# Masks in the slot of the scores, another order of the first transfers, and ScalarE's rounding of outputs ahead of weights

## The chip, the cores and the metric

The kernel runs on one core of one Trainium2 chip. The metric is the device time of one execution in microseconds (us); the median of three runs of the kernel before is 1189.74 us. Five engines work beside each other, each through its own instructions in order: TensorE (PE; its weight loads stand apart as PEld), VectorE (DVE), ScalarE (ACT), GpSimd (POOL) and SyncE (SP), which issues nearly all transfers.

## The reference

A retention layer is followed by two feed-forward layers:

```python
state = gamma * state + outer(k[t], v[t])      # per batch and head, 768 steps
y[t]  = scale * q[t] @ state
x  = y of 4 batches as 3072 tokens x 512
h  = x @ w_in   (512 x 2048);  g = h - tanh(h);                 x = g @ w_out
h  = x @ w_in2  (512 x 2048);  g = h if h > 0 else exp(h) - 1;  out = g @ w_out2
```

The weights arrive as 64-bit floats. The kernel reads each as two 32-bit words and makes a 32-bit float of them on the chip.

## The kernel before

**Retention.** The 3072 tokens are cut into 24 steps of 128 tokens; step s belongs to batch element s mod 4 and to chunk s // 4. For each step TensorE makes the scores of keys and queries into two PSUM banks (`att_scores`, L164), VectorE multiplies them by a causal mask with decay (L173, two instructions, tile `pt`) and, from chunk 1 on, scales the queries in place (`att_scale_q`, L135, tile `qk`). Then TensorE makes the outputs `o` (`att_out`): from chunk 1 on it first multiplies the scaled queries by the state (L187), then the masked scores by the values (L195). The result is split into a rounded half (ScalarE, L203) and a rest (VectorE, L204). The state is renewed by TensorE (L214, from keys that VectorE scaled, L149, tile `kn`) and VectorE (L237, L240; for chunk 0 one copy for two steps, L228). The outputs and the state's product use PSUM banks `a0` and `a1` that the scores of the next step use too.

**Feed-forward.** One iteration n handles one block of 512 tokens and one of 16 slices f of the hidden width. TensorE makes h by 12 matmuls (L251); ScalarE and VectorE turn h into v by a chain (ScalarE L271, L272, L274, L275; VectorE L277, L280, L283, L284 in the first layer); the next iteration splits v into g (ScalarE L260, VectorE L264); two iterations later TensorE adds the 12 matmuls of the second product (L317, `acc`).

**Weights.** A weight tile is fetched (L81, tile `raw`), ScalarE makes a float of its high word (L86, `convert_a`, into one of four buffers `w32`), VectorE brings in the low bits (L93, L94, `convert_b`), ScalarE rounds (L106, `convert_c`), and VectorE makes the rest (L107), which frees the `w32` buffer. Iterations 0 to 4 convert two tiles each, the later ones one, up to about iteration 23.

**What sets the order.** The program is written out by hand; every engine does its instructions in the order of the code. In an iteration VectorE's chain is interleaved with a list `side`: the rest of the previous g, then the conversions. Behind that list comes `att_scale_k` (L149), and then ScalarE is given the L86 of the next iteration's tiles. Scores of a step are a generator: TensorE's part runs in its iteration n, directly behind h; the part behind `yield`, the two masks and the scaled queries, runs at the head of iteration n + 1 (`for g in gens: run(g)`), so it stands on VectorE behind all of `side`. The step's outputs and state on TensorE stand in iteration n + 1 behind that iteration's h. Steps 5 to 7 have their scores in iterations 1, 3, 5; the others from iteration 22 on. Before the loop the four steps of chunk 0 and step 4's scores are written out one by one, with a few matmuls on zeros (`warm`) between. A transfer may be issued only when the one issued eight before it (SP's and ScalarE's counted together) has landed.

Of the kernel before, what the change touches and what calls it, by code (L numbers as in the profile page):

```python
# [40 lines left out]
def retention_moe_kernel(ctx: ExitStack, tc: tile.TileContext, dims, ins, out):  # L41
# [109 lines left out]
    def att_scores(s):  # L151
        t = qkv_t[s][0]
        if s < B:
            pt = tmp.tile([P, 2, NP, P], F32, tag="g", bufs=G_BUFS, name=f"pt{s}")
        else:
            pt = att1.tile([P, 2, NP, P], F32, tag="pt", name=f"pt{s}")
        sc = []
        for j in range(2):
            pool, tag = bank(s, f"sc{j}")
            sc.append(pool.tile([P, NP, P], F32, tag=tag, name=f"sc{s}_{j}"))  # L160
        for p in range(NP):
            for j in range(2):
                r = slice(j * D, (j + 1) * D)
                nc.tensor.matmul(  # L164
                    out=sc[j][:, p, :],
                    lhsT=t[r, 1, p * P:(p + 1) * P],
                    rhs=t[r, 0, p * P:(p + 1) * P],
                    start=True, stop=True,
                )
        pt_t[s] = pt  # L170
        yield
        for j in range(2):
            nc.vector.tensor_tensor(out=pt[:, j], in0=sc[j], in1=dtab[:, j], op=ALU.mult)  # L173
        if s >= B:
            att_scale_q(s)

    def att_out(s):
        t, v, _ = qkv_t[s]
# [193 lines left out]
    def run(g):  # L372
        for _ in g:
            pass
# [4 lines left out]
    with tc.manual_schedule():  # L379
# [22 lines left out]
        for s in range(B):  # L402
            att_load(s, qk0[s])
            att_load_v(s)
            if s % 2:
                fetch(*jobs0[s // 2])
        kn23 = att.tile([P, 2, TB], F32, tag="qk", name="kn23")
        for s in range(B):
            att_load_kn(s, kn23[:, s - 2, :] if s > 1 else None)
        fetch(*jobs0[2])  # L410
        fetch(*jobs0[3])
        att_load(B, att.tile([P, 2, TB], F32, tag="qk", name="qk4"))
        for job in jobs0[4:12]:
            fetch(*job)

        g_sc, g_out = {}, {}

# [19 lines left out]
        warm(3)  # L437
        scores_pe(1)
        warm(3)
        convert_a(jobs0[0])  # L440
        run(g_sc[0])
        out_pe(0)
        run(g_sc[1])
        ops(convert_b(jobs0[0]))
        lo0 = convert_c(jobs0[0])
        convert_a(jobs0[1])
        run(g_out[0])
        scores_pe(2)
        warm(3)
        out_pe(1)  # L450
        lo0()
        run(g_sc[2])
        ops(convert_b(jobs0[1]))
        run(g_out[1])
        lo1 = convert_c(jobs0[1])
        convert_a(jobs0[2])
        scores_pe(3)
        warm(3)
        out_pe(2)
        run(g_sc[3])  # L460
        lo1()
        run(g_out[2])
        convert_a(jobs0[3])
        out_pe(3)
        for s in range(B):
            att_scale_k(s)
        run(g_out[3])
        pairs = [att_state_pair(j) for j in range(2)]
        for g in pairs:
            next(g)  # L470
        for g in pairs:
            run(g)
        att_load_v(B)
        att_load_kn(B)
        scores_pe(B)
        ops(convert_b(jobs0[2]))
        run(g_sc[B])
        att_scale_k(B)
        ops(convert_b(jobs0[3]))

# [73 lines left out]
        for ph, b, f, flo, fhi in order:  # L554
# [6 lines left out]
            jobs = todo.get(n, [])  # L561
            h = first_mm(2 * ph, xhl[ph * NB + b], f, n)
            gens = []
            for g, *args in events.get(n, []):
                gens.append(g(*args))
                next(gens[-1], None)
            v, chain = (act_elu if ph else act_tanhshrink)(h, n, flush)
            halves = [convert_c(job) for job in prev_jobs]
            side = []
# [1 line left out]
            side += halves  # L571
            if prev_v is not None:
                side.insert(0, lambda: split_lo(g_t[n - 1], prev_v))
            interleave(chain, side)
            if n in scale_k:
                att_scale_k(scale_k[n])
# [83 lines left out]
```

## Time and profile before

| | |
|---|---|
| median of three runs | 1189.74 us (1189.67 to 1189.8) |
| the profiled execution | 1187.96 us |
| its span | 1186.2 us |
| TensorE matmuls busy | 1152.7 us, 97% |
| VectorE busy | 682.8 us, 58% |
| ScalarE busy | 624.0 us, 53% |
| mean granted clock of TensorE | 0.993 of full speed |
| chain that ended last | PE 83%, DVE 8%, issue 4%, ACT 2%, DMA 2% |

The span is the time from the first to the last instruction; the profiled execution's own time is 1.76 us longer. TensorE's sequence from about 97 us to the end is nearly gapless: h, second product, h, second product, with a retention step between now and then. Shares over the whole span say little about the first 97 us, where VectorE is busy nearly all the time and TensorE waits; those are read stretch by stretch.

### The profile page before, as it was taken

What the parts mean: (1) busy time and instruction counts of PE and PEld (TensorE: products, weight loads), DVE (VectorE), ACT (ScalarE), POOL (GpSimd) and SP (SyncE); (2) the same over time, 40 slices, a digit from 0 to 9 for tenths busy, and PEclk for the clock granted to TensorE, in tenths of its full rate; (3) what the DMA queues carried; (4) which work ended last, traced back from release to release, by engine and by line L of the source; (5) the groups of instructions that cost most, each with busy time, mean ns of one, the idle gap of its engine ahead of it and who ended that gap; (6) DMA issues with size and microseconds to landing.
All of it is one profiled execution on the core that took longest, in us unless ns stands there. A gap on an engine that the chain in (4) does not pass through costs nothing.

```text
span 1186.2 us, 15678 instructions
## 1 busy us (share of the span) xinstructions
PE 1152.7 (97%) x6038; PEld 943.5 (80%) x6039; DVE 682.8 (58%) x1133; ACT 624.0 (53%) x1097; POOL 5.6 (0%) x10
## 2 busy tenths in 40 slices
PE   7799999999999999999999999999999999999998
PEld 5577887787888887888888888888888888888886
DVE  4877887656665666666689766334343333333332
ACT  2456775454445454544678766444544444453534
POOL 0000000100000000000000000000000000000000
PEclk8899999999999999999999999999999999999999
DMA  9750030513103100200476400200200200200000
GB/s 355 296 227 19 18 107 27 116 36 71 53 19 107 36 28 1 89 28 1 145 229 196 141 1 1 71 1 1 72 1 1 72 1 1 72 1 1 36 1 36
DMA packets 27562, 80.44 MB, mean 68 GB/s; under 512 B 3168, under 2 KB 3168, under 8 KB 27488
## 3 DMA queue, kind: packets, MB, share of 16 engines
q1 hardware_dynamic: 26048, 76.56, 18.6%
q0 software_dynamic: 864, 2.10, 1.2%
q8 instruction: 47, 0.77, 0.3%
q10 hardware_dynamic: 576, 0.79, 0.2%
q14 instruction: 27, 0.22, 0.1%
HBM read 64.76 MB, written 14.68 MB: 67 GB/s over the span
## 4 chain that ended last, share of the span: by engine, by line
PE 83%; DVE 8%; issue 4%; ACT 2%; DMA 2%; ACTq 0%; DVEq 0%; SPq 0%
PE acc L317 41%; PE h L251 38%; PE o L187 2%; PE o L195 2%; DVE pt L173 2%; DVE v L284 1%; DVE kn L149 1%; ACT v L272 1%; DVE v L280 1%; DVE qk L135 1%; DVE h L283 1%; DMA kn<-qkv 1%; ACT u L271 1%; DMA raw<-w 1%; DMA gtab<-gtab 1%
## 5 line engine op out<-in xcount | busy, mean ns | idle before, releaser
L317 PE MATMUL acc<-g,w 128*128 128x512 f32 x1152 | 281.8, 393 | 0.0
L251 PE MATMUL h<-x,w 128*128 128x512 f32 x1152 | 277.7, 390 | 0.0
L317 PE MATMUL acc<-w,g 128*128 128x512 f32 x1152 | 276.7, 389 | 0.6 <-DVE g L264 0.6
L251 PE MATMUL h<-y,w 128*128 128x512 f32 x1152 | 276.7, 389 | 0.0
L317 PEld LDWEIGHTS acc<-w,g 128*128 128x128 f32 x1152 | 216.2, 188 | 45.8 <-DVE g L264 1.0
L251 PEld LDWEIGHTS h<-x,w 128*128 128x128 f32 x1152 | 216.5, 188 | 45.3 <-ACT w L106 0.2
L251 PEld LDWEIGHTS h<-y,w 128*128 128x128 f32 x1152 | 216.3, 188 | 44.8
L317 PEld LDWEIGHTS acc<-g,w 128*128 128x128 f32 x1152 | 213.4, 188 | 47.0 <-ACT g L260 0.7
L297 DVE SCALAR_TENSOR_TENSOR v<-v,t 128x512 f32<-128x512 f32 x96 | 66.5, 693 | 299.6 <-ACT t L295 299.6
L292 ACT ACTIVATE u<-h 128x512 f32<-128x512 f32 x96 | 57.4, 598 | 259.8 <-PE h L251 258.3
L271 ACT ACTIVATE u<-h 128x512 f32<-128x512 f32 x96 | 57.4, 598 | 245.8 <-issue 214.5
L277 DVE SCALAR_TENSOR_TENSOR v<-v,u 128x512 f32<-128x512 f32 x96 | 66.4, 692 | 161.4 <-ACT v L272 161.3
L264 DVE TENSOR_TENSOR g<-v,g 128x512 fp32r<-128x512 f32 x192 | 131.5, 685 | 0.8 <-ACT g L260 0.8
L260 ACT ACTIVATE g<-v 128x512 fp32r<-128x512 f32 x192 | 118.1, 615 | 2.0 <-DVE v L300 2.0
L284 DVE COPY_PREDICATED v<-m,h 128x512 f32<-128x512 uint16 x96 | 70.7, 736 | 6.0
L272 ACT ACTIVATE v<-u,qa_b 128x512 f32<-128x512 f32 x96 | 69.5, 724 | 3.2
L275 ACT ACTIVATE m<-u,xs_b 128x512 bf16<-128x512 f32 x96 | 68.2, 710 | 0.0
L283 DVE TENSOR_TENSOR h<-h,t 128x512 f32<-128x512 f32 x96 | 66.5, 693 | 0.0
L300 DVE TENSOR_TENSOR v<-h,v 128x512 f32<-128x512 f32 x96 | 65.7, 684 | 0.0
L280 DVE SCALAR_TENSOR_TENSOR v<-v,h 128x512 f32<-128x512 f32 x96 | 65.3, 681 | 0.0
L293 ACT ACTIVATE v<-u 128x512 f32<-128x512 f32 x96 | 60.6, 631 | 3.1
L295 ACT ACTIVATE t<-u 128x512 f32<-128x512 f32 x96 | 59.2, 617 | 0.0
(44 smaller groups left out, 605.2 us busy)
## 6 DMA issues: line engine op xcount, KB each, us to landing
raw<-w SPq DMA_DIRECT2D x64, 512.0 KB, 5.4
qk<-qkv SPq DMA_DIRECT2D x20, 512.0 KB, 4.7
v<-qkv SPq DMA_DIRECT2D x24, 256.0 KB, 6.1
x<-x1d SPq DMA_DIRECT2D x12, 512.0 KB, 5.8
kn<-qkv SPq DMA_DIRECT2D x20, 256.0 KB, 5.6
out<-o SPq DMA_DIRECT2D x10, 512.0 KB, 2.9
x1d<-o SPq DMA_DIRECT2D x8, 512.0 KB, 3.4
stage<-qkv SPq DMA_DIRECT2D x4, 512.0 KB, 6.8
```

Source lines behind the costliest of these rows:

```text
L251: nc.tensor.matmul(out=h, lhsT=w[:, a, c * P:(c + 1) * P], rhs=x[:, b, c, :], start=(i == 0), stop=(i == 3 * KC - 1),)
L260: nc.scalar.activation(out=t[:, 0, :], in_=g, func=AF.Copy)
L264: nc.vector.tensor_tensor(out=t[:, 1, :], in0=g, in1=t[:, 0, :].bitcast(F32), op=ALU.subtract)
L271: nc.scalar.activation(out=u, in_=h, func=AF.Square)
L272: nc.scalar.activation(out=v, in_=u, func=AF.Square, bias=qa_b)
L275: nc.scalar.activation(out=big, in_=u, func=AF.Relu, bias=xs_b)
L277: lambda: nc.vector.scalar_tensor_tensor(out=v, in0=v, scalar=QB, in1=u, op0=ALU.add, op1=ALU.mult),
L280: lambda: nc.vector.scalar_tensor_tensor(out=v, in0=v, scalar=C2, in1=h, op0=ALU.mult, op1=ALU.mult),
L283: lambda: nc.vector.tensor_tensor(out=h, in0=h, in1=th, op=ALU.subtract),
L284: lambda: nc.vector.copy_predicated(out=v, mask=big.bitcast(U16), data=h),
L297: lambda: nc.vector.scalar_tensor_tensor(out=v, in0=v, scalar=1.0, in1=th, op0=ALU.add, op1=ALU.mult),
L317: nc.tensor.matmul(out=acc[e], lhsT=lhsT, rhs=rhs, start=(f == lo and i == 0), stop=(f == hi - 1 and i == 2),)
```

## The change

Four things change in the code. (1) From chunk 1 on, the two masks and the scaling of the queries are no longer run at the head of the next iteration: they are put into `side` at its second place, so that VectorE does them between the instructions of the chain of the iteration that made the scores. (2) SyncE issues the second weight tile and all weight tiles after it later, behind the keys of the states and step 4's queries; the eight tiles from the fifth on come behind step 4's values and keys. (3) ScalarE's rounding of the first steps' outputs (L203) comes ahead of the conversion of the next weight tile (L86), and TensorE's scores and outputs of steps 2 and 3 move up. (4) Six matmuls on zeros are left out (two of four groups of three).

```diff
--- before.py
+++ after.py
@@ -168,11 +168,16 @@
                     start=True, stop=True,
                 )
         pt_t[s] = pt
-        yield
-        for j in range(2):
-            nc.vector.tensor_tensor(out=pt[:, j], in0=sc[j], in1=dtab[:, j], op=ALU.mult)
-        if s >= B:
-            att_scale_q(s)
+        masks = [
+            lambda j=j: nc.vector.tensor_tensor(out=pt[:, j], in0=sc[j], in1=dtab[:, j], op=ALU.mult)
+            for j in range(2)
+        ]
+        if s < B:
+            yield
+            for op in masks:
+                op()
+        else:
+            yield masks + [lambda: att_scale_q(s)]
 
     def att_out(s):
         t, v, _ = qkv_t[s]
@@ -402,16 +407,15 @@
         for s in range(B):
             att_load(s, qk0[s])
             att_load_v(s)
-            if s % 2:
-                fetch(*jobs0[s // 2])
+            if s == 1:
+                fetch(*jobs0[0])
         kn23 = att.tile([P, 2, TB], F32, tag="qk", name="kn23")
         for s in range(B):
             att_load_kn(s, kn23[:, s - 2, :] if s > 1 else None)
+        fetch(*jobs0[1])
+        att_load(B, att.tile([P, 2, TB], F32, tag="qk", name="qk4"))
         fetch(*jobs0[2])
         fetch(*jobs0[3])
-        att_load(B, att.tile([P, 2, TB], F32, tag="qk", name="qk4"))
-        for job in jobs0[4:12]:
-            fetch(*job)
 
         g_sc, g_out = {}, {}
 
@@ -437,44 +441,46 @@
         warm(3)
         scores_pe(1)
         warm(3)
-        convert_a(jobs0[0])
         run(g_sc[0])
         out_pe(0)
+        convert_a(jobs0[0])
         run(g_sc[1])
+        scores_pe(2)
+        run(g_out[0])
+        out_pe(1)
         ops(convert_b(jobs0[0]))
+        run(g_sc[2])
         lo0 = convert_c(jobs0[0])
+        run(g_out[1])
+        scores_pe(3)
+        out_pe(2)
+        lo0()
+        run(g_sc[3])
+        run(g_out[2])
+        out_pe(3)
+        att_scale_k(0)
+        att_scale_k(1)
+        run(g_out[3])
         convert_a(jobs0[1])
-        run(g_out[0])
-        scores_pe(2)
-        warm(3)
-        out_pe(1)
-        lo0()
-        run(g_sc[2])
-        ops(convert_b(jobs0[1]))
-        run(g_out[1])
-        lo1 = convert_c(jobs0[1])
-        convert_a(jobs0[2])
-        scores_pe(3)
-        warm(3)
-        out_pe(2)
-        run(g_sc[3])
-        lo1()
-        run(g_out[2])
-        convert_a(jobs0[3])
-        out_pe(3)
-        for s in range(B):
-            att_scale_k(s)
-        run(g_out[3])
+        att_scale_k(2)
+        att_scale_k(3)
         pairs = [att_state_pair(j) for j in range(2)]
         for g in pairs:
             next(g)
+        ops(convert_b(jobs0[1]))
+        lo1 = convert_c(jobs0[1])
+        convert_a(jobs0[2])
         for g in pairs:
             run(g)
+        lo1()
         att_load_v(B)
         att_load_kn(B)
-        scores_pe(B)
+        for job in jobs0[4:12]:
+            fetch(*job)
+        masks4 = next(att_scores(B))
+        convert_a(jobs0[3])
         ops(convert_b(jobs0[2]))
-        run(g_sc[B])
+        ops(masks4)
         att_scale_k(B)
         ops(convert_b(jobs0[3]))
 
@@ -561,9 +567,10 @@
             jobs = todo.get(n, [])
             h = first_mm(2 * ph, xhl[ph * NB + b], f, n)
             gens = []
+            masks = []
             for g, *args in events.get(n, []):
                 gens.append(g(*args))
-                next(gens[-1], None)
+                masks += next(gens[-1], None) or []
             v, chain = (act_elu if ph else act_tanhshrink)(h, n, flush)
             halves = [convert_c(job) for job in prev_jobs]
             side = []
@@ -571,6 +578,7 @@
             side += halves
             if prev_v is not None:
                 side.insert(0, lambda: split_lo(g_t[n - 1], prev_v))
+            side[1:1] = masks
             interleave(chain, side)
             if n in scale_k:
                 att_scale_k(scale_k[n])
```

SyncE, the first transfers behind `v3`: before, the second weight tile stands ahead of the keys `kn`, and the weights up to `raw1_4` stand ahead of `v4`.

```order
L130 DMA v3_134<-qkv 128x512
L81 DMA raw0_1_136<-w0 128x512
L142 DMA kn0_139<-qkv 128x512
L142 DMA kn1_141<-qkv 128x512
L142 DMA kn23_138<-qkv 128x512 x2
L81 DMA raw0_2_145<-w0 128x512
L81 DMA raw1_0_147<-w1 128x512
L125 DMA qk4_149<-qkv 128x1024
L81 DMA raw0_3_151<-w0 128x512
L81 DMA raw1_1_153<-w1 128x512
L81 DMA raw0_4_155<-w0 128x512
```

The same place now:

```order
L130 DMA v3_134<-qkv 128x512
L142 DMA kn0_137<-qkv 128x512
L142 DMA kn1_139<-qkv 128x512
L142 DMA kn23_136<-qkv 128x512 x2
L81 DMA raw0_1_143<-w0 128x512
L125 DMA qk4_145<-qkv 128x1024
L81 DMA raw0_2_147<-w0 128x512
L81 DMA raw1_0_149<-w1 128x512
L130 DMA v4_312<-qkv 128x512
L142 DMA kn4_314<-qkv 128x512
L81 DMA raw0_3_316<-w0 128x512
L81 DMA raw1_1_318<-w1 128x512
```

`raw0_1` went back by four transfers, `qk4` up; `v4` and `kn4`, which wait until TensorE has used step 0's buffers, now stand ahead of `raw0_3` and all that follow.

ScalarE, before the loop (x0: the rounded outputs, w32: the float of a weight tile, w: its rounded half); before:

```order
L86 ACTIVATE w32_0_0_195<-raw0_0_128 128x512
L106 ACTIVATE w0_0_213<-w32_0_0_195 128x512
L86 ACTIVATE w32_0_1_215<-raw0_1_136 128x512
L203 ACTIVATE x0_208<-o0_199 128x4x128
L203 ACTIVATE x0_208<-o1_233 128x4x128
L106 ACTIVATE w0_1_249<-w32_0_1_215 128x512
L86 ACTIVATE w32_0_2_251<-raw0_2_145 128x512
L203 ACTIVATE x0_208<-o2_267 128x4x128
L86 ACTIVATE w32_1_0_281<-raw1_0_147 128x512
L203 ACTIVATE x0_208<-o3_283 128x4x128
```

and now:

```order
L86 ACTIVATE w32_0_0_191<-raw0_0_128 128x512
L208 ACTIVATE x0_190<-o0_181 128x4x128
L106 ACTIVATE w0_0_221<-w32_0_0_191 128x512
L208 ACTIVATE x0_190<-o1_208 128x4x128
L208 ACTIVATE x0_190<-o2_236 128x4x128
L208 ACTIVATE x0_190<-o3_250 128x4x128
L86 ACTIVATE w32_0_1_263<-raw0_1_143 128x512
L106 ACTIVATE w0_1_305<-w32_0_1_263 128x512
L86 ACTIVATE w32_0_2_307<-raw0_2_147 128x512
L86 ACTIVATE w32_1_0_343<-raw1_0_149 128x512
```

All four roundings of outputs moved ahead of the L86 that waits for `raw0_1`.

VectorE in iteration 1 (v1: the chain's tile, pt5 and qk5: masks and queries of step 5, w32 and w: conversions); before:

```order
L93 TENSOR_SCALAR w32_0_4_433<-w32_0_4_433 128x512
L283 TENSOR_TENSOR h0_1_447<-h0_1_447,t1_472 128x512
L93 TENSOR_SCALAR w32_1_2_435<-w32_1_2_435 128x512
L284 COPY_PREDICATED v1_473<-m1_474,h0_1_447 128x512
L94 SCALAR_TENSOR_TENSOR w32_0_4_433<-raw0_4_155,w32_0_4_433 128x512
L94 SCALAR_TENSOR_TENSOR w32_1_2_435<-raw1_2_157,w32_1_2_435 128x512
L107 TENSOR_TENSOR w0_3_481<-w32_0_3_359,w0_3_481 128x512
L107 TENSOR_TENSOR w1_1_483<-w32_1_1_361,w1_1_483 128x512
L149 TENSOR_TENSOR kn5_365<-kn5_365,ktab_89 128x512
L173 TENSOR_TENSOR pt5_460<-sc5_0_461,dtab_88 128x512
L173 TENSOR_TENSOR pt5_460<-sc5_1_462,dtab_88 128x512
L135 TENSOR_TENSOR qk5_363<-qk5_363,qtab_87 128x512
```

and now:

```order
L172 TENSOR_TENSOR pt5_454<-sc5_0_455,dtab_88 128x512
L288 TENSOR_TENSOR h0_1_441<-h0_1_441,t1_466 128x512
L172 TENSOR_TENSOR pt5_454<-sc5_1_456,dtab_88 128x512
L289 COPY_PREDICATED v1_467<-m1_468,h0_1_441 128x512
L135 TENSOR_TENSOR qk5_357<-qk5_357,qtab_87 128x512
L93 TENSOR_SCALAR w32_0_4_427<-w32_0_4_427 128x512
L93 TENSOR_SCALAR w32_1_2_429<-w32_1_2_429 128x512
L94 SCALAR_TENSOR_TENSOR w32_0_4_427<-raw0_4_320,w32_0_4_427 128x512
L94 SCALAR_TENSOR_TENSOR w32_1_2_429<-raw1_2_322,w32_1_2_429 128x512
L107 TENSOR_TENSOR w0_3_475<-w32_0_3_353,w0_3_475 128x512
L107 TENSOR_TENSOR w1_1_477<-w32_1_1_355,w1_1_477 128x512
L149 TENSOR_TENSOR kn5_359<-kn5_359,ktab_89 128x512
```

The masks and the scaled queries moved from behind L149 to between the chain's instructions; the conversions and L149 moved back by the same three instructions.

## Rows read from the trace of the kernel before

**Rows 1.** Waits of TensorE, whole run: who for whom, us, times, longest.

```profile
PE o L187 <- DVE qk L135: 16.2, 15, 2.9
```

**Rows 2.** Timeline, iterations 1 to 7: start, us, engine, instruction, [idle before <- releaser].

```profile
45.28 2.93 PE L164 MATMUL sc<-qk 64*128 64x128 f32 x16 [4.77 <-DVE x L204]
...
46.00 0.68 DVE L277 SCALAR_TENSOR_TENSOR v<-v,u 128x512 f32<-128x512 f32 x1
...
51.60 1.27 ACT L86 ACTIVATE w<-raw 128x512 f32<-128x512 f32 x2 [3.21 <-DVE w L107]
...
54.49 0.69 DVE L277 SCALAR_TENSOR_TENSOR v<-v,u 128x512 f32<-128x512 f32 x1
...
54.72 1.09 PE L187 MATMUL o<-qk,st 64*64 64x128 f32 x16 [2.91 <-DVE qk L135]
...
63.01 0.42 DVE L240 TENSOR_TENSOR st<-ds,st 128x256 f32<-128x256 f32 x1
...
72.91 0.68 DVE L277 SCALAR_TENSOR_TENSOR v<-v,u 128x512 f32<-128x512 f32 x1
...
73.13 1.75 PE L187 MATMUL o<-qk,st 64*64 64x128 f32 x16 [2.81 <-DVE qk L135]
...
80.82 0.42 DVE L240 TENSOR_TENSOR st<-ds,st 128x256 f32<-128x256 f32 x1
...
92.20 1.09 PE L187 MATMUL o<-qk,st 64*64 64x128 f32 x16 [2.45 <-DVE qk L135]
...
94.71 3.02 PE L317 MATMUL acc<-g,w 128*128 128x512 f32 x12
```

**Rows 3.** Timeline of TensorE: two later outputs.

```profile
190.71 1.09 PE L187 MATMUL o<-qk,st 64*64 64x128 f32 x16 [1.90 <-DVE qk L135]
...
237.41 1.09 PE L187 MATMUL o<-qk,st 64*64 64x128 f32 x16 [0.56 <-DVE qk L135]
```

**Rows 4.** Timeline of VectorE ahead of that last output.

```profile
231.56 0.70 DVE L277 SCALAR_TENSOR_TENSOR v<-v,u 128x512 f32<-128x512 f32 x1 [3.93 <-ACT v L272]
...
234.16 0.74 DVE L284 COPY_PREDICATED v<-m,h 128x512 f32<-128x512 uint16 x1
...
235.38 1.28 DVE L173 TENSOR_TENSOR pt<-sc,dtab 128x512 f32<-128x512 f32 x2
236.58 0.68 DVE L135 TENSOR_TENSOR qk<-qk,qtab 128x512 f32<-128x512 f32 x1
```

**Rows 5.** Timeline of all engines before the loop and in iteration 0.

```profile
13.80 1.16 PE L164 MATMUL sc<-stage 64*128 64x128 f32 x16 [2.09 <-DMA stage<-qkv]
...
15.86 1.98 PE L195 MATMUL o<-pt,v 128*64 128x128 f32 x16
...
17.47 0.66 ACT L86 ACTIVATE w<-raw 128x512 f32<-128x512 f32 x1 [3.59 <-DMA raw<-w]
...
18.65 0.69 DVE L204 TENSOR_TENSOR x<-o,x 128x512 fp32r<-128x512 f32 x1 [5.50 <-ACT x L203]
...
29.41 0.69 DVE L228 COPY st<-dsp 128x512 f32<-128x512 f32 x1 [0.61 <-PE dsp L214]
...
31.24 3.02 PE L251 MATMUL h<-x,w 128*128 128x512 f32 x12
...
34.30 0.60 ACT L271 ACTIVATE u<-h 128x512 f32<-128x512 f32 x1 [6.86 <-PE h L251]
...
36.08 0.69 DVE L149 TENSOR_TENSOR kn<-kn,ktab 128x512 f32<-128x512 f32 x1 [3.05 <-DMA kn<-qkv]
...
37.76 0.68 DVE L277 SCALAR_TENSOR_TENSOR v<-v,u 128x512 f32<-128x512 f32 x1
```

**Rows 6.** The page's costliest groups: instruction, xcount | busy us, mean ns | idle before.

```profile
L272 ACT ACTIVATE v<-u,qa_b 128x512 f32<-128x512 f32 x96 | 69.5, 724 | 3.2
```

**Rows 7.** All 64 transfers of weight tiles, from issue to landing.

```profile
DMA to landing us min/median/max: 3.4/5.4/10.6
```

**Rows 8.** One stretch by engine: us, busy, granted clock (PEclk), DMA share, GB/s.

```profile
70.00:80.00 10.00, 7.19 (x62) 6.04 (x61) 9.37 (x17) 6.28 (x11) 0.00 (x0) 0.83 0.68 277
```

## The prediction

> **What bounds the kernel now.** I read the waits of TensorE first, then the timeline around the longest of them, then the chain back to what each one waits for. The kernel is TensorE's from about 97 us on, so only time in which TensorE stands still, or is held back before that, can be won. The list of its waits has one large entry: the outputs' matmuls (L187) wait 15 times, 16.2 us in all, for VectorE's scaling of the queries (L135) [rows 1]. Three of these are long and early, 2.91, 2.81 and 2.45 us [rows 2], 8.2 together; the other twelve, 8.0 us, are one of 1.90 in iteration 23 and eleven of about 0.56 [rows 3]. Of the 20 outputs in the loop the remaining five don't wait.
>
> The late ones are plain: VectorE goes through its chain, then the keys (L149), two masks, and the queries, which end at 237.26; the output starts 0.15 later [rows 3, 4]. VectorE stood idle 3.93 us before that chain, so here only the order is at fault.
>
> The first 97 us are another matter. Before the loop ScalarE stands in front of L86 until a weight tile lands (3.59 us, until 17.47), the rounding of outputs is queued behind it, and VectorE waits 5.50 us for that rounding, until 18.65 [rows 5]. Later the keys of step 4 land late (VectorE waits 3.05 us, until 36.08), so that the first chain starts at 37.76 though ScalarE began on h0 at 34.30 [rows 5]. Then follows a ring: ScalarE's L86 waits for a buffer that VectorE's L107 frees at the end of its list (3.21 us, until 51.60), and the next h's activations, so the next chain, are queued behind L86 [rows 2].
>
> **The change part by part.** I call the start of iteration n's chain on VectorE c(n). VectorE starts one instruction of this size every 0.60 us (the two masks and the queries: 1.20 from 235.38 to 236.58 [rows 4]); L93 I take as half of that, 0.34.
>
> *Late outputs.* The masks and queries come before L149, which then stands behind them, so the queries are done 0.60 earlier, at 236.66, and the output could start at 236.81. TensorE is free at 237.41 - 0.56 = 236.85 [rows 3]. The wait goes, narrowly; the chain's last instruction began 0.19 late in the old order (234.16 plus 0.60 is 234.76, but the masks now fill what it waited for), which widens the margin. What is late next is nothing: TensorE follows on itself. The chain itself ends 1.0 to 1.2 us later, in front of a ScalarE that needs it only behind the next h's first two activations. In iteration 23 VectorE's list still has one conversion; that moves behind the queries, which saves more than the 1.90. Twelve waits of 8.0 us, and about 0.03 each for the refilling of TensorE: 8.4 us. Bounds: 8.4, and 1.9 if the margin of 0.04 is not met anywhere but in iteration 23.
>
> *Before the loop.* Scores 2 start at 13.80 as now (their transfer keeps its place) and end at 14.96. With no matmuls on zeros behind them, outputs 1 follow, 1.98 at worst, until 16.9 [rows 5]; ScalarE rounds them at once, and VectorE has them from 17.5 on. Then its list runs: outputs 1, L107, masks 3, outputs 2, two keys, outputs 3, two keys, L93 and L94 of the second tile: eleven of 0.60 and one of 0.34, with some 0.3 of waits for scores 3, to 24.7. TensorE's state product follows the last key by about 1 us (an estimate: half as many columns as the outputs' 1.98). The two copies of the state come next, the second at 25.3 instead of 29.41 [rows 5]: 4.1 earlier. From it to h0 it is 1.83, from there 3.06 to ScalarE's first activation [rows 5]: h0 at 27.1, ScalarE at 30.2. VectorE meanwhile does a mask pair, the queries and step 4's keys. These keys and values are issued when TensorE has used step 0's buffers, about 22.6 and 23.0, with the queue almost run dry, since eight weight tiles no longer stand ahead of them; at the 5.4 us of a usual tile [rows 7] they are there at 28.4, before VectorE asks (29.4). The tile that ScalarE must turn before it may start on h0, `raw1_1`, is issued at 23.8 and there at 29.2. c(0) is 1.4 behind ScalarE's start (0.60 and 0.72 [rows 5, 6] and the hand-over), at 31.6 instead of 37.76: 6.2 us. Step 5's queries stand behind the eight tiles on SyncE; they are issued once `raw0_3` has landed, about 29, and even the longest landing, 10.6 [rows 7], has them there just when scores 5 want them. Bounds: if `raw1_1` takes that longest landing, ScalarE starts at 35.0 and c(0) at 36.4, a gain of 1.4; if outputs 1 run at 1.09, 0.9 more than 6.2, so 7.1.
>
> *Iterations 0 to 6.* Here the masks move ahead of conversions, and behind those conversions stands the ring with ScalarE. I follow it from c(0) = 31.6. c(1) is 8.24 later as now (37.76 to 46.00), 39.8. Scores 5 wait for VectorE's release of the banks and end at 42.0 (now 48.21, 6.2 later), so the first mask waits 0.4 on VectorE, which has chain, conversions and keys queued behind it. Mask, chain, mask, chain, queries end at 45.2; the outputs start there instead of 54.72 - 6.2 = 48.5. But L107, the last of its list, is 2.2 later than now, with it ScalarE's L86 pair (51.60 - 6.2 + 2.3 = 47.7), with it the activations of h2: the pair takes 1.2 and the two activations 1.4, so c(2) is at 50.3, where 54.49 - 6.2 = 48.3 would be no loss. A new wait comes too: the state product needs the keys of L149, now behind the conversions, done at 49.0. So h3 starts at 52.5, and the bank for scores 6 is released by L240, 8.94 behind c(2) (54.49 to 63.43 [rows 2]), at 59.2: TensorE waits there for 3.9. Iteration 3 repeats iteration 1: queries done at 64.1, TensorE ready at 66.1, so no wait; L86 at 66.7, c(4) at 69.2 (2.5 late). L240 is 8.33 behind c(4) (72.91 to 81.24): 77.5, and scores 7 wait 3.1 for it. After that TensorE is never held: second product 78.6, h6 81.4, outputs 84.2 (VectorE's queries done at 82.4), next second product at 86.8. Now it starts at 94.71: 7.9 earlier, of which 6.2 are from before the loop. So the early three waits of 8.2 bring 1.8, the rest comes back as later releases of the banks. Bounds: 8.2 if none comes back, and -1.6 if each stall of TensorE is followed by a slow stretch of 1.7 (below), twice.
>
> Sum: 6.2 + 1.8 + 8.4 = 16.4. The profiled execution of 1187.96 (span 1186.2) would be 1171.6; the median of the runs is 1.78 above the profiled execution, so 1173.3.
>
> **A rule against it.** After the wait of 2.81 the outputs took 1.75 instead of 1.09, and the stretch from 70 to 80 us has a granted clock of 0.83, a part of it at the lower of the two levels, 1.2 instead of 2.4 GHz [rows 2, 8]; that cost 1.7 us of ten. The Trainium skill says in "TensorE: Matmul & The Clock Gate" (Part 1: The HAM clock gate) that half rate is the default state and activity releases it. Six of the warming matmuls are gone, so by that rule the opening would be slower than I have it, and the whole about 1178 instead of 1173.3; the trace agrees that a standstill can be followed by the low level, yet after 2.91 and 2.45 the outputs kept 1.09 [rows 2]. Hence a rival of its own.
>
> **The rivals.**
> - *Low clock in the opening.* h0 at half clock is 2.7 us longer (3.02 now, at full), which delays c(0) by as much; a slow stretch after each of two stalls adds 1.7 or, where VectorE is late anyway, less: about 5 together, 1178. For it: fewer matmuls on zeros, the 0.83. Against it: TensorE's real work before h0 is denser than now.
> - *Weights late.* Tiles behind step 4's keys land as slowly as the slowest now, the reordering only moves the wait from keys to tiles: 1.4 in place of 6.2, total 11.6, so 1178.1. Against it: all those transfers are issued earlier than VectorE's need by 5 us or more.
> - *All waits go.* The early three pay in full, 8.2 for 1.8: 1166.9. Against it: VectorE has next to no idle time between c(1) and L107 of iteration 1, and L86 waits for its end [rows 2].
> - *VectorE held by the scores: slower.* The mask now stands inside the chain, in order, and waits for TensorE's scores, as it will by 0.4 in iteration 1. If all 20 masks held VectorE by w and TensorE lost w each time, the sum is 16.4 - 20w: from w = 0.82 on it is slower, at w = 2 it is 1213. Against it: from iteration 22 on scores run while ScalarE does two activations and VectorE three instructions, with 3.93 idle [rows 4].
>
> **How the numbers follow.** Forecast 0.62, low clock 0.12, late weights 0.14, all waits go 0.08, slower 0.04. The bounds added up would give 1166.0 and 1188.0, but need every term at its end at once; the range goes from near the third rival (1167.5) to just beyond the first two (1180). Within 0.2% (2.4 us, about what a measurement of this kernel can tell from no change) needs the opening to lose what the late outputs give: 0.02, out of late weights. Faster 0.94, slower 0.04.
>
> **What would show it.** Right: no wait of L187 for L135 from iteration 22 on; c(0) near 31.6; ScalarE's roundings of x0 end before its second L86; new waits of TensorE for L240 and L149 in iterations 1 to 5, some 8 us together; the second product of iteration 6 near 86.8. Wrong: L187 still waiting 0.1 or more late in the run; ScalarE waiting for a weight tile beyond 30; c(0) later than 34; a granted clock well under 0.9 between 27 and 60; a wait of a mask for scores beyond iteration 5.

## The result and the profile after

The changed kernel takes 1172.41 us, the median of four runs (1170.16 to 1172.87); the kernel before took 1189.77 beside it (four runs). The ratio is 0.9847, with a 95% interval of 0.983 to 0.9864. The forecast was 1173.3. The profiled execution took 1170.16 (span 1168.3), 17.8 less than the one of before; it is the fastest of the four.

In the changed kernel the lines from L187 on have numbers five higher (L187 is L192, L204 is L209, L240 is L245, L277 is L282); those up to L164 kept theirs, and the masks are L172.

The page: busy time of each engine; the chain that ended last; and the row that answers to [rows 6].

```profile
PE 1151.0 (99%) x6033; PEld 941.6 (81%) x6033; DVE 681.2 (58%) x1133; ACT 624.1 (53%) x1097; POOL 5.6 (0%) x10
...
PE 93%; DVE 3%; ACT 1%; DMA 1%; issue 1%; SPq 0%; DVEq 0%; ACTq 0%
...
L277 ACT ACTIVATE v<-u,qa_b 128x512 f32<-128x512 f32 x96 | 69.4, 723 | 3.2
```

No engine's busy time fell by more than 1.7 us. TensorE's share of the ending chain rose from 83 to 93%: only standstill went. Which standstill shows in the waits of TensorE (who for whom, us, times, longest), the answer to [rows 1].

```profile
PE sc L164 <- DVE x L209: 7.4, 3, 3.5
...
PE sc L164 <- DVE st L245: 0.8, 2, 0.4
```

The 16.2 us of outputs that waited for scaled queries are gone. What has grown is the wait of the scores for VectorE to release the banks (L209 and, right behind it, L245): 8.2 us together in iterations 1, 3 and 5. The first of them is not new: scores 5 waited 4.77 before [rows 2] and wait 3.51 now.

The timeline before the loop and in iteration 0 answers to [rows 5].

```profile
13.70 1.16 PE L164 MATMUL sc<-stage 64*128 64x128 f32 x16 [0.55 <-DMA stage<-qkv]
14.79 1.09 PE L200 MATMUL o<-pt,v 128*64 128x128 f32 x16
20.50 0.60 ACT L208 ACTIVATE x<-o 128x512 fp32r<-128x512 f32 x1 [1.85 <-PE o L200]
21.09 0.70 ACT L86 ACTIVATE w<-raw 128x512 f32<-128x512 f32 x1
24.00 1.28 DVE L233 COPY st<-dsp 128x512 f32<-128x512 f32 x2
28.66 0.69 DVE L149 TENSOR_TENSOR kn<-kn,ktab 128x512 f32<-128x512 f32 x1
30.86 0.69 DVE L282 SCALAR_TENSOR_TENSOR v<-v,u 128x512 f32<-128x512 f32 x1 [0.45 <-ACT v L277]
```

All four roundings of outputs are over before ScalarE turns the second weight tile (21.09), the two copies of the state start from 24.00 on (the second stood at 29.41), step 4's keys are scaled without a wait for a transfer (L149, 28.66), and the first chain starts at 30.86 in place of 37.76. In the chain of waits (start, us, what) ScalarE's way to h0 ends with a weight tile, `raw1_1`, issued at 22.62 (forecast 23.8) and there at 28.7 (29.2):

```profile
22.62 6.10 DMA raw<-w
28.80 0.67 ACT w L86
```

The 64 weight tiles landed as they did before ([rows 7] had 3.4, 5.4 and 10.6):

```profile
DMA to landing us min/median/max: 3.3/5.6/10.5
```

Iterations 1 to 6, the answer to [rows 2]:

```profile
38.40 2.93 PE L164 MATMUL sc<-qk 64*128 64x128 f32 x16 [3.51 <-DVE x L209]
41.27 4.56 PE L256 MATMUL h<-x,w 128*128 128x512 f32 x12
45.76 1.09 PE L192 MATMUL o<-qk,st 64*64 64x128 f32 x16
46.57 1.30 ACT L86 ACTIVATE w<-raw 128x512 f32<-128x512 f32 x2 [5.05 <-DVE w L107]
49.13 0.69 DVE L282 SCALAR_TENSOR_TENSOR v<-v,u 128x512 f32<-128x512 f32 x1 [1.39 <-ACT v L277]
57.27 0.49 PE L164 MATMUL sc<-qk 64*128 64x128 f32 x2 [3.06 <-DVE x L209]
66.46 1.09 PE L192 MATMUL o<-qk,st 64*64 64x128 f32 x16
67.95 0.69 DVE L282 SCALAR_TENSOR_TENSOR v<-v,u 128x512 f32<-128x512 f32 x1 [1.39 <-ACT v L277]
75.51 0.48 PE L164 MATMUL sc<-qk 64*128 64x128 f32 x2 [0.80 <-DVE x L209]
83.15 1.09 PE L192 MATMUL o<-qk,st 64*64 64x128 f32 x16
85.66 3.02 PE L322 MATMUL acc<-g,w 128*128 128x512 f32 x12
```

The three outputs (45.76, 66.46, 83.15) no longer wait. ScalarE's L86 waits longer than it did (5.05, was 3.21), and with it the chains of iterations 2 and 4 come late; TensorE meets that as the waits at 57.27 and 75.51. The wait at 38.40 lies ahead of these chains. The second product of iteration 6 starts at 85.66, 9.05 before the 94.71 of before.

Late in the run (TensorE's rows; answer to [rows 3]) the output of the 237.41 of before follows 2.81 behind the start of h, with no idle time, and VectorE (answer to [rows 4]) has the queries ahead of the keys:

```profile
221.98 2.88 PE L256 MATMUL h<-x,w 128*128 128x512 f32 x12
224.79 1.09 PE L192 MATMUL o<-qk,st 64*64 64x128 f32 x16
...
223.80 0.68 DVE L135 TENSOR_TENSOR qk<-qk,qtab 128x512 f32<-128x512 f32 x1
224.39 0.68 DVE L149 TENSOR_TENSOR kn<-kn,ktab 128x512 f32<-128x512 f32 x1
```

The clock, by stretches (us, busy time of PE, PEld, DVE, ACT, POOL with instructions, granted clock, DMA share, GB/s); the second row answers to [rows 8].

```profile
37.00:45.00 8.00, 6.53 (x26) 5.25 (x27) 7.24 (x14) 4.49 (x9) 0.00 (x0) 0.57 1.03 413
...
70.00:80.00 10.00, 8.82 (x48) 6.93 (x47) 9.27 (x18) 6.26 (x12) 0.00 (x0) 1.00 0.00 0
```

The low clock that stood between 70 and 80 is gone there; between 37 and 45 most of the time is at 1.2 GHz, after TensorE stood still for 3.51 us. Behind the second standstill (3.06, until 57.27) the second product took 3.76 at 60.05, against 3.02 at full clock.

### The profile page after: what moved, and what is told of

The parts are those of the page before. It is cut to its first block, busy times and chain, and to the rows that moved or that the text cites. A ratio compares the mean times of both kernels' runs of the same rounds, so it can differ in the third digit from the quotient of the medians.

```text
span 1168.3 us, 15675 instructions
## 1 busy us (share of the span) xinstructions
PE 1151.0 (99%) x6033; PEld 941.6 (81%) x6033; DVE 681.2 (58%) x1133; ACT 624.1 (53%) x1097; POOL 5.6 (0%) x10
## 3 DMA queue, kind: packets, MB, share of 16 engines
q1 hardware_dynamic: 26048, 76.56, 18.7%
## 4 chain that ended last, share of the span: by engine, by line
PE 93%; DVE 3%; ACT 1%; DMA 1%; issue 1%; SPq 0%; DVEq 0%; ACTq 0%
PE acc L322 44%; PE h L256 43%; PE sc L164 2%; PE o L200 2%; PE o L192 1%; PE ds L219 1%; DVE w L94 1%; DMA raw<-w 1%; DVE w L107 1%; DMA stage<-qkv 0%; DVE x L209 0%; DVE v L289 0%; DVE v L285 0%; ACT w L86 0%; DVE h L288 0%
## 5 line engine op out<-in xcount | busy, mean ns | idle before, releaser
L282 DVE SCALAR_TENSOR_TENSOR v<-v,u 128x512 f32<-128x512 f32 x96 | 66.4, 692 | 152.7 <-ACT v L277 152.6
L277 ACT ACTIVATE v<-u,qa_b 128x512 f32<-128x512 f32 x96 | 69.4, 723 | 3.2
```

Source lines behind the costliest of these rows:

```text
L277: nc.scalar.activation(out=v, in_=u, func=AF.Square, bias=qa_b)
L282: lambda: nc.vector.scalar_tensor_tensor(out=v, in0=v, scalar=QB, in1=u, op0=ALU.add, op1=ALU.mult),
```

## The experiments

The theory: three gains that add up. The opening brings c(0) some 6 us forward; the masks late in the run bring all they waited; the early masks bring little, because their wait comes back through L107, L86 and the release of the banks. The rivals are named in the expectations. The kernels ran in three sets, each beside runs of the kernel before on the same chip (medians 1188.54, 1189.48 and 1189.85). Within a set I compare medians, across sets ratios.

**The change again.** The same kernel, in the first set.

> The changed kernel again, as a measure beside the three others on the same chip: 1172.4; both theories the same. In the trace: whether the low granted clock at 37 to 45 us comes again.

Measured: 1171.33 (1171.04 to 1172.75), ratio 0.9849, 0.9835 to 0.9863. Its profile has c(0) at 31.81, a microsecond later than the first one, with the same distances from there on (c(2) at 50.08, c(4) at 68.90). Its outputs 1 took 1.98, not 1.09:

```profile
14.80 1.98 PE L200 MATMUL o<-pt,v 128*64 128x128 f32 x16
```

Everything up to c(0) moves back with them (the copies of the state start at 24.94, not 24.00). So these two profiles of one kernel differ by about 1 us through TensorE's clock at 15 us, and the forecast's c(0) of 31.6, worked out with 1.98, is the right one for the second.

**Masks alone.** The new slot of the masks, with transfers, zeros and ScalarE's order of before:

```diff
-            if s == 1:
-                fetch(*jobs0[0])
+            if s % 2:
+                fetch(*jobs0[s // 2])
...
-        fetch(*jobs0[1])
-        att_load(B, att.tile([P, 2, TB], F32, tag="qk", name="qk4"))
         fetch(*jobs0[2])
         fetch(*jobs0[3])
+        att_load(B, att.tile([P, 2, TB], F32, tag="qk", name="qk4"))
+        for job in jobs0[4:12]:
+            fetch(*job)
...
+        convert_a(jobs0[0])
         run(g_sc[0])
         out_pe(0)
-        convert_a(jobs0[0])
...
```

> Opening and transfers as before; only the masks and the scaled queries stand in the slot of their own iteration. Theory (late outputs 8.85 us as measured in the changed kernel, iterations 0 to 6 worth about 2 more because the early waits mostly come back as later releases of the banks): about 11 us off 1189.8, 1179. Rival (all fifteen waits of the outputs pay in full, and the opening adds nothing): 16 us, 1173.5. In the trace: no wait of the outputs for the queries' scaling, and c(0), the start of VectorE's first chain, still at 37.8.

Measured: 1177.53 (1176.64 to 1178.0), ratio 0.9898, 0.9884 to 0.9912: 11.0 us. c(0) is that of before:

```profile
37.93 0.68 DVE L282 SCALAR_TENSOR_TENSOR v<-v,u 128x512 f32<-128x512 f32 x1
```

The forecast's share for the masks was 1.8 + 8.4 = 10.2. The rival, in which all waits go, is out.

**Opening alone.** The new opening; every mask in its old slot:

```diff
+            ops(late)
+            late = []
...
-                masks += next(gens[-1], None) or []
+                todo_masks = next(gens[-1], None) or []
+                if True:
+                    late += todo_masks
...
```

> The new opening and transfers; masks and queries of steps 5 to 23 at the head of the next iteration as before. Theory: c(0) moves from 37.8 to 30.9, and those 6.9 us stay to the end: 1183. Rival (the early start is swallowed by VectorE, which bounds iterations 0 to 6 anyway): 1187 to 1189.8. In the trace: the three early waits of the outputs near 2.9, 2.8 and 2.5 stay, and the twelve late ones.

Measured: 1181.63 (1180.66 to 1185.43), ratio 0.9937, 0.9921 to 0.9953: 6.9 us, with c(0) at 31.59, 6.17 earlier than before. The wait of the outputs is back as it was in [rows 1]:

```profile
PE o L192 <- DVE qk L135: 15.8, 15, 3.4
```

The two halves give 11.0 and 6.9, sum 17.9; the whole gives 17.2 in the same set. They add up within the measurement. The profiled execution of the opening alone took 1183.39: behind a wait of 1.88, at 48.58, its outputs ran at a low clock, 1.54 and 1.97 instead of 1.09 each.

**Late masks only.** The new opening; the old slot is kept for the masks of iterations 1, 3 and 5 alone (`if n < NF:` in place of `if True:`).

> The changed kernel, but with masks and queries in the old place in iterations 1, 3 and 5 (steps 5 to 7), in the new one from iteration 22 on. Theory (the new slot is worth 2.1 us there, the rest of the 8.2 comes back): 1174.5. Rival A (the ring of conversions makes the new slot harmful there): 1170.5. Rival B (worth the full 8.2): 1180.6.

Measured: 1173.05 (1172.9 to 1173.2), ratio 0.9861, 0.9848 to 0.9875. So the three early masks bring 1173.05 - 1171.33 = 1.7 us and the late ones 1181.63 - 1173.05 = 8.6. Its waits:

```profile
PE o L192 <- DVE qk L135: 8.2, 3, 2.9
PE sc L164 <- DVE x L209: 4.4, 1, 4.4
```

With the old slot the early waits are 8.2 and 4.4; with the new one 7.4, all at L209. Part of the 8.2 comes back as releases of the banks, part as slower work of TensorE (h2 took 4.56 in the change, 3.66 here), and only 1.7 is left over. This kernel also shows what the new slot does to VectorE's chains, since it has the same opening and c(0) = 31.77:

```profile
48.52 0.68 DVE L282 SCALAR_TENSOR_TENSOR v<-v,u 128x512 f32<-128x512 f32 x1
```

With the old slot c(2) is 16.75 behind c(0), as before (16.73); with the new one 18.27.

Its opening has something else to tell. Outputs 1 took 1.09 and h0 began at 26.47, as in the first profile of the change, yet c(0) is not at 30.86, because ScalarE had to turn a late weight tile first:

```profile
29.81 0.68 ACT L86 ACTIVATE w<-raw 128x512 f32<-128x512 f32 x1 [0.63 <-DMA raw<-w]
```

ScalarE began on h0 at 30.40, 0.92 behind its end (29.48).

**Zeros back.** Two of the removed groups of three matmuls on zeros stand again behind scores 2 and 3:

```diff
         scores_pe(2)
+        warm(3)
...
         scores_pe(3)
+        warm(3)
```

> The changed kernel with the two groups of three matmuls on zeros back, behind scores 2 and scores 3. Theory (TensorE has the full clock from 10 to 37 us without them, the low level at 37 to 45 comes from the standstill just before it): no gain, 0 to 1 us more, 1171.5 to 1172.5. Rival (the missing zeros cost the clock in the opening): 1.7 to 3.4 us less, 1168 to 1169.7, and a clock near 0.9 at 37 to 45.

Measured: 1173.91 (1173.32 to 1176.55), ratio 0.9876, 0.986 to 0.9891; against the 0.9849 of the change about 3 us slower, though the intervals overlap a little. Neither expectation had that. The timeline tells why:

```profile
15.26 1.46 PE L392 MATMUL warmp<-warm 128*128 128x512 bf16 x3
16.64 1.85 PE L200 MATMUL o<-pt,v 128*64 128x128 f32 x16
...
18.54 0.60 ACT L208 ACTIVATE x<-o 128x512 fp32r<-128x512 f32 x1 [3.51 <-PE o L200]
...
34.49 0.69 DVE L282 SCALAR_TENSOR_TENSOR v<-v,u 128x512 f32<-128x512 f32 x1 [1.37 <-ACT v L277]
```

Outputs 1 stand behind the zeros, still run at a low clock, and ScalarE rounds them at 18.54 (16.83 in the second run of the change); c(0) is 2.7 later than there: 1.8 from these outputs (h0 starts at 29.14, not 27.36), 0.9 from the last weight tile, which ScalarE turned only at 32.55. The theory's full clock from 10 to 37 us holds for the first profile of the change, not for the second, which has 0.68 between 15 and 20, as this kernel has.

**Transfers of before.** The order of ScalarE and the missing zeros are kept; the queue is that of before (the diff of the transfers shown with the masks alone).

> The changed kernel with SyncE's first transfers in the old order: second weight tile ahead of the keys, eight weight tiles ahead of step 4's values and keys. Theory (step 4's keys then land near 34 as they did at 36, VectorE waits for them): c(0) at 35.5, about 4.7 later, 1176. Rival (the transfers were hidden, all of the opening's gain is ScalarE's order): 1171.4.

Measured: 1177.91 (1177.29 to 1178.21), ratio 0.9903, 0.989 to 0.9917: 0.0054 or 6.4 us more than the change. Step 4's values and keys stand behind eight weight tiles. TensorE waits for the values, VectorE for the keys, and behind the keys stands the first chain: c(0) is at 37.98, though ScalarE began on h0 at 29.28.

```profile
35.69 1.97 PE L200 MATMUL o<-pt,v 128*64 128x128 f32 x16 [5.42 <-DMA v<-qkv]
36.31 0.69 DVE L149 TENSOR_TENSOR kn<-kn,ktab 128x512 f32<-128x512 f32 x1 [7.80 <-DMA kn<-qkv]
```

**ScalarE's order of before.** The new transfers, but ScalarE turns the second weight tile ahead of the first outputs:

```diff
         scores_pe(2)
+        convert_a(jobs0[1])
         run(g_out[0])
...
         run(g_out[3])
-        convert_a(jobs0[1])
```

> The changed kernel, but ScalarE turns the second weight tile ahead of the first outputs' rounding, as before. Theory (ScalarE stands until that tile lands, 20.5 us, and VectorE's list behind the first outputs' rest starts at 21.8 instead of 13.8): c(0) about 7 later, 1178. Rival (VectorE's list has slack to hide it, or the weights would be waited for anyway): 1171.4 to 1173.

Measured: 1180.59 (1179.24 to 1182.58), ratio 0.9928, 0.9915 to 0.9941: 9.4 us more.

```profile
21.97 0.66 ACT L86 ACTIVATE w<-raw 128x512 f32<-128x512 f32 x1 [10.01 <-DMA raw<-w]
22.53 0.58 ACT L208 ACTIVATE x<-o 128x512 fp32r<-128x512 f32 x1
```

ScalarE stands in front of a tile that now comes behind the states' keys (though still ahead of step 4's queries) and is turned only at 21.97, and the rounding waits behind it; c(0) is at 40.59, 8.8 later. Beside the 0.9898 of the masks alone, ScalarE's new order without the transfers has 0.9903 and the transfers without ScalarE's order 0.9928: the gain needs both.

**Rounding later.** Inside the loop L86 moves from the end of an iteration to the head of the next, behind L208:

```diff
+            if n:
+                for job in jobs:
+                    convert_a(job)
             h = first_mm(2 * ph, xhl[ph * NB + b], f, n)
...
-            for job in todo.get(n + 1, []):
-                convert_a(job)
```

> The changed kernel, and inside the loop too ScalarE rounds the outputs (L208) ahead of the next weight tiles' L86: these move to the head of the next iteration. Theory (in iterations 1, 3 and 5 the banks for the scores come free only behind an L208 that is queued behind L86; VectorE idles 1.21, 1.21 and 0.63 us before L209): TensorE's waits for L209 fall from 7.4 by about 3, total 1.5 to 2.5 us less, 1169. Rival (L86 and the activations of h behind it bound the ring, not L208): no change, 1171.4.

Measured: 1170.52 (1169.19 to 1171.17), ratio 0.9841, 0.9827 to 0.9855: about 1 less, not told apart from the change. In the profile the loop did gain what the theory said, 2.2 us from c(0) to the second product of iteration 6 (52.58, 54.78 in the second run of the change), but c(0) was 0.4 later (32.17), so the whole doesn't show it clearly. The wait at L209 shrank as expected, but one for step 5's queries took its place:

```profile
PE sc L164 <- DMA qk<-qkv: 3.4, 1, 3.4
...
PE sc L164 <- DVE x L209: 2.4, 2, 1.7
```

**Subtractions first.** If the late chains hang on the ring L107, L86, activations, freeing the buffers earlier must help. VectorE's L107 stands ahead of L94:

```diff
-            interleave_into(side, [convert_b(j) for j in jobs])
-            side += halves
+            low = [convert_b(j) for j in jobs]
+            side = [x[0] for x in low] + halves + [x[1] for x in low]
```

> On VectorE the three subtractions of an iteration that empty the buffers of rounded-off halves stand ahead of the three half additions. Theory: from iteration 2 to 5 ScalarE's weight pieces wait for these buffers (5.05 us at 46.57 in the changed kernel), and TensorE's rows scores<-x wait 7.4 us in three places for what comes behind them on ScalarE and VectorE. With the buffers free some 1.4 us earlier the waits for x shrink from 7.4 to about 4 to 5 us, and the time to about 1169 (2 to 3 less than 1171.4). Rival: the waits end with something else behind x (the bank's release, a transfer of the stage), and the time stays within 0.5 of 1171.4.

Measured: 1166.11 (1165.24 to 1167.13), ratio 0.98, 0.9787 to 0.9814: by the ratios 5.8 us less than the change, and 5.2 less than the change with busy matmuls that ran in the same set (below). That is twice what was expected, and this version beats both kernels. ScalarE's waits for L107 fell from

```profile
ACT w L86 <- DVE w L107: 19.0, 5, 5.1
```

in the change to

```profile
ACT w L86 <- DVE w L107: 13.2, 6, 4.4
```

and the first row of the next fence answers to c(2) at 49.13: VectorE stands idle 0.19 ahead of it, not 1.39, and it is 16.44 behind c(0), not 18.27.

```profile
48.18 0.69 DVE L282 SCALAR_TENSOR_TENSOR v<-v,u 128x512 f32<-128x512 f32 x1 [0.19 <-ACT v L277]
...
80.62 0.69 DVE L282 SCALAR_TENSOR_TENSOR v<-v,u 128x512 f32<-128x512 f32 x1 [0.55 <-ACT v L277]
```

TensorE's waits for x are 1.2, under the 4 to 5 expected, though step 5's queries are late here too:

```profile
PE sc L164 <- DMA qk<-qkv: 3.4, 1, 3.4
...
PE sc L164 <- DVE x L209: 1.2, 2, 0.7
```

From c(0) at 31.74 to c(6) it is 48.9 us; in the second run of the change 53.8 (31.81 to 85.62). The expectation had counted 1.4 in two iterations; the rows have 1.18 in iteration 0, 0.65 in 1, 1.19 in 2 and in 3, and the rest in 4 and 5. The Trainium skill says in "Perfetto Trace Analysis" (Optimization Strategy) that a gap that repeats can mean too few buffers. The trace agrees that the gap is one of buffers, four of them; here freeing them sooner shortened it, from 19.0 to 13.2 in all. No run had more buffers, and none had the subtractions first with the masks in their old slot.

**The three together.** Subtractions first, rounding later, and step 5's queries and keys sent ahead of six weight tiles:

```diff
-        for job in jobs0[4:12]:
+        for job in jobs0[4:6]:
+            fetch(*job)
+        att_load(B + 1, att.tile([P, 2, TB], F32, tag="qk", name="qk5"))
+        att_load_kn(B + 1)
+        for job in jobs0[6:12]:
             fetch(*job)
```

> Three edits on the changed kernel: the subtractions ahead of the half additions, the weight pieces rounded at the head of the next iteration behind x, and step 5's queries and keys sent ahead of six weight pieces, so that the wait for them (3.4 us when only the rounding was moved) goes. Theory: waits for x fall under 3 us, no wait for queries and keys, time 1167 to 1168.5. Rival: the six weight pieces now land later and their rounding waits instead, so that the sum is that of moving the rounding alone, about 1170.5.

Measured: 1165.3 (1164.47 to 1166.7), ratio 0.9794, 0.9781 to 0.9808: below the expected range, but not told apart from the subtractions alone. The wait for queries is gone; the waits for x are 3.9, not under 3.

**Busy in the standstill.** Three matmuls on the mask table, read by nobody, in iteration 1 ahead of scores 5:

```diff
+            if n == 1:
+                idle = ps_acc.tile([P, NP, P], F32, tag="acc3", name="idle")
+                for _ in range(3):
+                    nc.tensor.matmul(out=idle, lhsT=dtab[:, 0, 0, :], rhs=dtab[:, 0], start=True, stop=True)
```

> Three matmuls on the mask table, whose result nobody reads, run on TensorE in iteration 1 between the hidden product and the scores of step 5, where it stands still for 3.5 us in the changed kernel before its clock is 0.57 for the window 37 to 45. Theory: the clock there stays near 1 and the 12 matmuls of the next hidden product take about 2.9 instead of 4.56 us, but the 1.7 us go into a longer wait behind them, since VectorE and ScalarE set the pace in iterations 2 to 5: time 1171 to 1171.5. Rival: TensorE's clock sets the pace there, and the time falls by the 1.7 us to about 1169.7.

Measured: 1171.26 (1170.86 to 1172.7), ratio 0.9845, 0.9832 to 0.9859: no change. The clock did what was wanted, the next h took 2.99 in place of 4.56, and the chain behind it, c(2), stayed (50.08 in the second run of the change):

```profile
37.00:45.00 8.00, 5.93 (x32) 3.73 (x30) 6.68 (x13) 5.38 (x10) 0.00 (x0) 1.00 1.01 406
```

```profile
47.90 0.68 DVE L149 TENSOR_TENSOR kn<-kn,ktab 128x512 f32<-128x512 f32 x1
48.68 0.69 PE L219 MATMUL ds<-v,kn 128*64 128x64 f32 x16 [1.52 <-issue]
...
49.95 0.69 DVE L282 SCALAR_TENSOR_TENSOR v<-v,u 128x512 f32<-128x512 f32 x1 [1.37 <-ACT v L277]
```

The faster h only brought TensorE to the state product (L219) before its keys: it stood 1.52 there, until 0.10 behind the end of L149 (the profile puts that to "issue"). In the change, at the low clock, it came there just as the keys were ready.

Added to the three edits, the same matmuls change nothing either:

> The three edits of the kernel with subtractions first, later rounding and earlier queries and keys, and the three idle matmuls in iteration 1. Theory: with the waits of VectorE and ScalarE shortened, the higher clock counts for a part of its 1.7 us: 0.5 to 1.5 less than the same kernel without the idle matmuls, 1166 to 1168. Rival: no difference between the two.

Measured: 1165.27 (1164.56 to 1166.38), ratio 0.9794, 0.978 to 0.9807. Here the rival was right: the clock between 37 and 45 us went from 0.59 to 1.00, and even with VectorE's and ScalarE's waits shortened that is worth nothing in that place.

## Why the prediction was right

The profiles can be cut in three: up to c(0), from there to the second product of iteration 6, and from there to the end (us).

| kernel | c(0) | to the second product of iteration 6 | to the end |
|---|---|---|---|
| before | 37.76 | 56.95 | 1091.5 |
| the change, two profiles | 30.86, 31.81 | 54.80, 54.78 | 1082.6, 1082.7 |
| masks alone | 37.93 | 54.79 | 1082.7 |
| opening alone | 31.59 | 58.48 | 1091.5 |
| late masks only | 31.77 | 56.95 | 1082.7 |
| subtractions first | 31.74 | 49.85 | 1082.6 |

In these kernels each edit moves its own column and leaves the others, but for the loop of the opening alone, whose slow outputs were named above. (With the transfers or ScalarE's order of before the loop has 55.5 and 56.0.) Each row is one profile, so a microsecond in the first two columns can be the clock of that execution.

*Late outputs.* Forecast 8.4, measured 8.6 by the difference of two kernels, and 17.9 - 9.05 = 8.85 from the two profiles (17.9 is the difference of the spans, 9.05 that of iteration 6's second product); the last column has it in every kernel. No row showed the forecast's 0.03 for the refilling of TensorE; 8.85 for 8.0 of waits is 0.07 each. The margin of 0.04 us was met everywhere, with 0.16 at the output shown (224.48 plus the hand-over of 0.15, against 224.79): no output waits for its queries from iteration 22 on.

*Before the loop.* Forecast 6.2; the first profile has 6.9 (30.86), the others 5.95 and 6.17 (31.81 and 31.59). Between the two profiles of the change the difference is the clock of outputs 1, for which the forecast took the slow value and set 7.1 as its bound. Both reasons that it named are shown: with the transfers of before c(0) is at 37.98, with ScalarE's order of before at 40.59.

*Iterations 0 to 6.* Forecast 1.8; measured 1.7 by the old slot for the early masks, and 9.05 - 6.9 = 2.15 from the profiles. The step behind the forecast, that L107 comes later and brings L86 and c(2) late, is in the rows: c(2) at 49.13 is 18.27 behind c(0) (16.73 before, 18.7 forecast). Two kernels with the same opening show the ring to be the cause: with the old slot for the early masks it is 16.75, with the new slot and the buffers freed earlier 16.44, and that kernel gains 5 to 6 us. The second product of iteration 6 was forecast at 86.8 and came at 85.66: 0.7 of that from c(0), 0.4 from the loop.

*What it had wrong.* The list of signs had new waits for L240 and L149, "some 8 us together", and the trace has 8.2 for L209 (which stands just ahead of L245) and L245. That the two agree is luck. Of the 8.2, 3.51 are the wait of scores 5, which stood before. Scores 6 waited 3.4 (forecast 3.9), scores 7 only 1.2 (forecast 3.1), mostly because slow matmuls brought TensorE there a microsecond later than forecast. The wait for the keys of L149 did not come, since h2 ended later than I had it: it ran at the low clock. With the clock at 1.00 the wait is there, 1.52. The first mask, forecast to wait 0.4 for scores 5, did not: it needs only the first of their two banks, and starts at 40.96, before the scores end (41.3). That is the 0.4 by which c(2) was forecast too late.

The list of signs also had "a granted clock well under 0.9 between 27 and 60" as one that would make the forecast wrong. It was 0.57 between 37 and 45, and the forecast held: the kernel with the clock at 1.00 there has the same time, because TensorE then waits for VectorE's keys. The bound had priced a slow stretch at 1.7 without asking what bounds the stretch; the rival's own words, "or, where VectorE is late anyway, less", are what happened. Two small slips change nothing: half of 0.60 for L93 is 0.30, not 0.34, and h0 at half clock would be 3.0 longer, not 2.7.

*The rivals.* Low clock in the opening: h0 took 3.02 and 3.03 in the two profiles, full clock, and the slow outputs 1 were in the sum. The zeros were no loss to leave out; with them c(0) is later. By the Trainium skill, "TensorE: Matmul & The Clock Gate" (Part 1: The HAM clock gate), half rate is what TensorE falls back to unless it is busy; the trace agrees on the clock (0.57 behind the standstill, 1.00 with the standstill filled), and the time didn't follow it. Weights late: one tile was there only at 28.7, but in the change it cost nothing; ScalarE began on h0 3.05 us after TensorE did (26.42, 29.47), as before (31.24, 34.30). It had nothing to spare, though: in the kernel with the late masks only, with the same opening, the tile held ScalarE up by 0.9. So this rival shows in some kernels, at a microsecond and not at the 4.8 that it was given. All waits go: out by the 1.7. Held by the scores: no sign of it in the change; the mask of iteration 1 starts 0.63 behind the instruction ahead of it, where 0.60 is VectorE's usual step. With the subtractions first, where step 5's queries came late, it waited 0.52.

## What to carry to other kernels

When an instruction that another engine waits for stands behind conversions, moving it ahead pays in full only where its engine has idle time ahead of that work; where the engine is busy, ask what the work that moved back was releasing, and reorder that too (subtractions first gave 5 to 6 us, more than the early masks did). In an opening, an in-order engine and the transfer queue have to be reordered together: either alone left c(0) where it was or later. Price a low clock only in a stretch where TensorE is the last to arrive: at 41 us it cost nothing, since VectorE's keys came no earlier; at 48 us in the opening alone, where the rest waited for the slow outputs, the loop of its profile was 1.5 us longer.

## What the runs showed of the hardware

Two groups of three warming matmuls cost more than they gave: the first took 1.46 us, the outputs behind it still took 1.85 (1.09 at full clock), and everything on ScalarE and VectorE that hung on those outputs came later. The same opening, run twice, had outputs 1 at 1.09 and at 1.98 us, which is the 1 us between two profiles of the same kernel. What decides between the two stays open: TensorE had stood still for 0.55 us ahead of scores 2 in the fast one and for 2.00 in the slow one, but in the kernel with the late masks only it stood 2.36 and outputs 1 took 1.09.
